# An attention stage's second product in column tiles of 32, with the sums as products of their own

## The chip, the cores and the metric

The kernel runs on one core of a Trainium2 chip. The metric is device time in microseconds (us) of one execution; a kernel's time is the median of its runs.

## What is computed

Attention over 2 batches of 12 heads, 448 positions and 64 values a head, with a soft cap on the scores, and then two feed-forward layers on the 896 tokens of 768 values. All inputs are 4-byte floats.

```
scores = (q @ k.T) / sqrt(64)            # per batch and head, 448 x 448
scores = cap * tanh(scores / cap)
attn   = exp(scores - max(scores)); attn = attn / (sum(attn) + 1e-9)
x      = attn @ v                        # heads joined: 896 x 768
h = x @ w_in;  x = (h * cos(h)) @ w_out      # 768 -> 2048 -> 768
h = x @ w_in2; out = (h * sigmoid(h)) @ w_out2
```

## The kernel before, in words

The order of the work on every engine is written out by hand; a tile framework adds the semaphores. After the attention stage come four projections (`gemm_in`, `gemm_out`, `gemm_in`, `gemm_last`), three matmuls for each product of split operands. Weights are prepared one after the other by `w_guard`, `w_floor`, `w_bits`, `w_hi` and `w_lo`; the first few of these steps are spread over the attention loop (the table `early`).

Attention works on 12 pairs of heads (`NPT`). A pair's two heads lie one above the other: head u of a pair takes rows 64u to 64u+63 of q and k, both stored with the 64 values of a head along the partitions and the positions along the free axis. Keys are the rows of a score tile, queries its 448 columns, so that the tile can be used as it stands in the second product. 448 keys make three whole tiles of 128 and a rest of 64 for each head; the rests of the two heads share one tile of 128 rows, the last keys (t = 3), in which k is stored so that the other head's rows are zero.

One turn of the loop over p (line 341) does the following.

- `load(p+3)` on GpSimd's queue and `load_v(p+1)` on SP's bring q and k (`raw`, three buffers) and v (`vf`).
- `S_pe(p+1, t)` on TensorE: q and k have been split into a high part `qh` and a low part `ql` of a reduced 4-byte type (`qk_split`, VectorE), and a score tile is three matmuls: high-high, high-low, low-high. For t = 0 to 2 each head has its own (64 rows, line 225, the two heads side by side), for t = 3 the two share one of 128 rows (line 228). Score tiles lie in three buffers of two banks each (`ps_s`), taken in turn, so that t = 3 takes the buffer of t = 0 of the same pair.
- `S_tanh(p+1, t)` and `S_exp(p+1)` on ScalarE write `e32`, seven chunks of 128 keys: chunk 2t+u for head u, chunk 6 for the last keys of both.
- `PV_mixed(p)`, between `S_pe(p+1, 2)` and `S_pe(p+1, 3)`, and `PV(p, u, ...)` at the turn's end are the second product, in plain 4-byte floats. Each head has its own accumulator (`po0`, `po1`, one bank each). The stationary operand is 128 columns wide: 64 values of v and, beside them, 64 columns of ones that were set once (`v_init`, GpSimd), so that the other half of the accumulator holds the sums of the exponentials, 64 times. Head u takes chunks u, u+2, u+4 with 128 rows and its 64 rows of chunk 6 in `PV_mixed`.
- `evac(p, u)` copies an accumulator to `xu` (VectorE, line 269) and sends one row of sums by SP's queue (line 271) to a small tile.
- `recip(p-2)`: reciprocal of the sums (line 277), to memory and back as a broadcast (`rs`, `rb`; lines 279 and 282, SP's queue). `norm_mul(p-3)` and `norm_split(p-3)` (lines 290, 297, 298, VectorE) multiply and split the result into `x`, which the first projection reads.

In the last turn there are no scores; `recip(10)` is brought forward, and the steps of pairs 9 to 11 follow the loop (lines 363 to 368). The first projection, `gemm_in`, reads batch 0 first (pairs 0 to 5) for two column tiles of the weights, then batch 1 without its last two pairs, and then pairs 10 and 11.

In a profile a 4-byte matmul of line 255 is two records of TensorE (and two weight loads), a matmul of the reduced type is one.

Of the kernel before, what the change touches and what calls it, by code (L numbers as in the profile page):

```python
# [25 lines left out]
F32 = mybir.dt.float32  # L28
F32R = mybir.dt.float32r
# [7 lines left out]
def tile_attention_ffn_ffn(  # L37
# [120 lines left out]
    with ExitStack() as actx:  # L158
# [5 lines left out]
        NCH = 7  # L164
        VW = 3 * D
        KB = S + 64
        QK = S + KB
        FIRST = S + P
        PAD = 16

        raw, vf = {}, []


        def v_init():
            for n in range(2):
                t = ap_.tile([P, NCH, VW], F32, name=f"vf{n}", bufs=1)
                nc.gpsimd.memset(t, 1.0)
                vf.append(t)

# [14 lines left out]
        def load_v(p):  # L194
            if p >= NPT:
                return
            nc.sync.dma_start(vf[p % 2][:, :, D:2 * D], qkv[p][:, PAD + QK:].rearrange("p (c d) -> p c d", d=D))

        qh, ql = {}, {}

        def qk_split(p, part=slice(0, QK)):
            if p >= NPT:
                return
            if p not in qh:
                qh[p] = ap_.tile([P, QK], F32R, tag="qh", name=f"qh{p}", bufs=2)
                ql[p] = ap_.tile([P, QK], F32R, tag="ql", name=f"ql{p}", bufs=2)
# [6 lines left out]
        def S_pe(p, t):  # L213
# [3 lines left out]
            sc[p, t] = ps  # L217
            h, l = qh[p], ql[p]
# [24 lines left out]

        po_ = {}
        wide = [slice(D, 3 * D), slice(0, 2 * D)]


        def PV(p, u, chunks):
            first = (p, u) not in po_
            if first:  # L250
                po_[p, u] = ps_o.tile([P, 512], F32, tag=f"po{u}", name=f"po{p}_{u}")[:, :S]
            for n, c in enumerate(chunks):
                rows = slice(0, P) if c < NCH - 1 else slice(u * D, (u + 1) * D)
                last = c < NCH - 1 and c >= NCH - 3
                nc.tensor.matmul(po_[p, u], vf[p % 2][rows, c, wide[u]], e32[p][rows, c, :], start=first and n == 0, stop=last)  # L255

        def PV_mixed(p):
            for u in range(2):
                PV(p, u, [NCH - 1])

        xu, sums, rb = {}, {}, {}

        def evac(p, u):
            if p < 0:
                return
            if u == 0:
                xu[p] = ap2.tile([P, 2, S], F32, tag="xu", name=f"xu{p}", bufs=4)
                sums[p] = ap2.tile([32, S // 16], F32, tag="sums", name=f"sums{p}", bufs=2)
            nc.vector.tensor_copy(xu[p][:, u], po_.pop((p, u)))
            row = D if u == 0 else 0  # L270
            nc.sync.dma_start(sums[p][16 * u:16 * u + 16], xu[p][row:row + 1, u, :])

        def recip(p):
            if p < 0:
                return
            s = sums.pop(p)
            nc.vector.reciprocal(out=s, in_=s)
            d = dpool.tile([2, S], F32, tag="rs", name=f"rs{p}")
            nc.sync.dma_start(d.rearrange("h (a n) -> (h a) n", a=16), s)
            r = ap2.tile([P, S], F32, tag="rb", name=f"rb{p}", bufs=4)  # L280
# [36 lines left out]
        nc.vector.memset(zero.bitcast(F32), 0.0)  # L317
        warm_up(8, ps_o.tile([P, 512], F32, tag="po1", name="warm0")[:, :S])

# [3 lines left out]
        get_scap(raw[0][:, :1])  # L323
        qk_split(0, slice(FIRST, QK))
        load(1)
# [11 lines left out]
        qk_split(1)  # L337
        warm_up(4, ps_o.tile([P, 512], F32, tag="po1", name="warm1")[:, :S])
        for u in range(2):
            PV(0, u, range(u, 4, 2))  # L340
        for p in range(NPT):
# [285 lines left out]
```

## Time and profile before

| | us |
|---|---|
| median of 3 runs | 579.0 (578.89 to 579.34) |
| the profiled execution | 579.33 |
| its span | 577.6 |
| TensorE busy | 571.5 (99%) |
| VectorE busy | 387.0 (67%) |
| ScalarE busy | 265.8 (46%) |
| GpSimd busy | 158.0 (27%) |
| granted clock of TensorE, mean over the span | 1.0 |

The span runs from the first instruction to the end of the last; the execution's own time is 1.7 us longer. Attention takes about the first 106 us of the span, the four projections the rest. A record of TensorE lasts longer than the distance to the next one, because matmuls are pipelined; the distance is what counts in a sum.

### The profile page before, as it was taken

The page shows a single profiled execution, that of the slowest core. Times are in us where ns is not written, and L with a number is a line of the kernel's source. Part 1 is how long each engine was busy: PE and PEld are TensorE (multiplying, and loading weights), DVE is VectorE, ACT ScalarE, POOL GpSimd, SP SyncE. Part 2 cuts the span into 40 slices and gives each one's busy share as a digit, 9 for nine tenths or more (in the row PEclk, how much of TensorE's full clock was granted, in tenths as well). Part 3 has the DMA queues.
Part 4 walks back from the last instruction along what each step waited for, and adds up shares of the span by engine and source line. Part 5 has one row for each costly group of instructions (what it writes and reads, how often), then busy time and mean ns, then how long its engine had stood idle before and what let it go on. Part 6 is the DMA issues. An engine that isn't in the chain of part 4 may idle for free.

```text
span 577.6 us, 7312 instructions
## 1 busy us (share of the span) xinstructions
PE 571.5 (99%) x2856; PEld 502.1 (87%) x2856; DVE 387.0 (67%) x490; ACT 265.8 (46%) x307; POOL 158.0 (27%) x81
## 2 busy tenths in 40 slices
PE   8999999999999999999999999999999999999997
PEld 5656655799999999999999999999999999999997
DVE  4358885599988898667646552888877776654501
ACT  5988888167777766223223222443333323232101
POOL 3001100033444433242332221344332323413300
PEclk9999999999999999999999999999999999999999
DMA  9236532123433333343433330343333334444102
GB/s 327 70 99 173 178 115 64 50 81 103 135 120 110 109 92 100 105 143 97 133 107 110 106 119 40 111 138 136 110 109 110 110 110 128 145 135 132 48 1 95
DMA packets 27201, 65.04 MB, mean 113 GB/s; under 512 B 14176, under 2 KB 17760, under 8 KB 27168
## 3 DMA queue, kind: packets, MB, share of 16 engines
q1 hardware_dynamic: 25728, 57.51, 31.9%
q0 software_dynamic: 1152, 6.78, 3.4%
q8 instruction: 22, 0.36, 0.2%
q10 hardware_dynamic: 288, 0.30, 0.2%
q14 instruction: 11, 0.09, 0.0%
HBM read 61.74 MB, written 2.80 MB: 112 GB/s over the span
## 4 chain that ended last, share of the span: by engine, by line
PE 98%; DMA 1%; DVE 0%; issue 0%; ACT 0%
PE h L397 40%; PE y L397 20%; PE o L544 20%; PE po L255 11%; PE sc L225 4%; PE sc L228 2%; DMA raw<-in_qkv 1%; PE warm L305 0%; DVE ql L209 0%; DVE qh L208 0%; DVE os L567 0%; ACT os L566 0%; DVE capt L71 0%
## 5 line engine op out<-in xcount | busy, mean ns | idle before, releaser
L119 POOL TENSOR_SCALAR w<-w 128x768 f32<-128x768 f32 (+1 forms) x63 | 148.4, 2355 | 312.5 <-ACT w L113 248.5
L397 PE MATMUL h<-x,whi 128*128 128x448 f32 x768 | 218.4, 366 | 0.0
L397 PEld LDWEIGHTS h<-x,whi 128*128 128x128 f32 x768 | 144.2, 188 | 11.8 <-issue 0.4
L397 PE MATMUL h<-x,wlo 128*128 128x448 f32 x384 | 140.2, 365 | 0.0
L143 ACT ACTIVATE whi<-w 128x768 fp32r<-128x768 f32 (+1 forms) x66 | 54.3, 822 | 143.2 <-DVE w L135 132.6
L544 PE MATMUL o<-whi,g 128*128 128x384 f32 x448 | 113.9, 335 | 0.0
L397 PE MATMUL y<-g,whi 128*128 128x448 f32 x384 | 109.3, 366 | 0.0
L132 DVE SCALAR_TENSOR_TENSOR w<-w,wraw 128x768 int32<-128x768 int32 (+1 forms) x66 | 61.5, 932 | 43.8 <-POOL w L119 42.9
L150 DVE TENSOR_TENSOR wlo<-w,whi 128x768 fp32r<-128x768 f32 (+1 forms) x66 | 61.4, 931 | 31.6 <-ACT whi L143 30.8
L544 PEld LDWEIGHTS o<-whi,g 128*128 128x128 f32 x448 | 81.0, 188 | 0.0
L397 PEld LDWEIGHTS y<-g,whi 128*128 128x128 f32 x384 | 72.1, 188 | 5.9
L397 PEld LDWEIGHTS h<-x,wlo 128*128 128x128 f32 x384 | 72.1, 188 | 5.7
L544 PE MATMUL o<-wlo,g 128*128 128x384 f32 x224 | 74.9, 335 | 0.0
L397 PE MATMUL y<-g,wlo 128*128 128x448 f32 x192 | 70.2, 366 | 0.0
L255 PE MATMUL po<-e,vf 128*128 128x448 f32 (+1 forms) x192 | 68.3, 541 | 1.0 <-issue 1.0
L135 DVE SCALAR_TENSOR_TENSOR w<-wraw,w 128x768 uint32<-128x768 uint32 (+1 forms) x66 | 61.6, 934 | 2.3
L130 DVE TENSOR_SCALAR wraw<-wraw 128x768 int32<-128x768 int32 (+1 forms) x66 | 55.9, 846 | 9.0 <-ACT w L113 9.0
L113 ACT ACTIVATE w<-wraw 128x768 f32<-128x768 f32 (+1 forms) x66 | 57.9, 877 | 2.7 <-DMA wraw<-in_moe_w_out 2.7
L255 PEld LDWEIGHTS po<-e,vf 128*128 128x128 f32 (+1 forms) x192 | 31.9, 189 | 25.9 <-issue 24.3
L236 ACT ACTIVATE e<-sc,scap 128x896 f32<-128x896 f32 (+1 forms) x48 | 40.8, 912 | 15.8 <-PE sc L225 11.8
L544 PEld LDWEIGHTS o<-wlo,g 128*128 128x128 f32 x224 | 42.1, 188 | 0.0
L453 ACT ACTIVATE r<-h 128x896 f32<-128x896 f32 (+1 forms) x18 | 14.8, 836 | 58.7 <-PE h L397 56.8
(53 smaller groups left out, 411.4 us busy)
## 6 DMA issues: line engine op xcount, KB each, us to landing
wraw<-in_moe_w_in SPq DMA_DIRECT2D x29, 768.0 KB, 4.3
wraw<-in_moe_w_out SPq DMA_DIRECT2D x22, 768.0 KB, 4.4
wraw<-in_moe_w_out SPq DMA_DIRECT2D x12, 640.0 KB, 4.1
raw<-in_qkv POOLq DMA_DIRECT2D x9, 480.0 KB, 6.3
vf<-in_qkv SPq DMA_DIRECT2D x12, 224.0 KB, 2.9
rb<-rs SPq DMA_DIRECT2D x24, 112.0 KB, 2.9
out<-os SPq DMA_DIRECT2D x13, 192.0 KB, 1.9
wraw<-in_moe_w_in POOLq DMA_DIRECT2D x3, 768.0 KB, 5.1
```

What stands on the lines that cost most here:

```text
L113: nc.scalar.activation(out=w32[i][:, :n, :].bitcast(F32), in_=wraw[i][:, :n, :, 1].bitcast(F32), func=AF.Abs, scale=2.0 ** -48)
L119: eng.tensor_scalar(out=t, in0=t, scalar1=2.0 ** -63, scalar2=None, op0=ALU.max)
L130: nc.vector.tensor_scalar(out=w1, in0=w1, scalar1=-0x80000000, scalar2=None, op0=ALU.bitwise_and)
L132: nc.vector.scalar_tensor_tensor(out=t, in0=t, scalar=3, in1=w1, op0=ALU.logical_shift_left, op1=ALU.bitwise_or)
L135: nc.vector.scalar_tensor_tensor(out=t, in0=w0.bitcast(U32), scalar=29, in1=t, op0=ALU.logical_shift_right, op1=ALU.bitwise_or)
L143: nc.scalar.activation(out=whi[i][:, :n, :], in_=w32[i][:, :n, :].bitcast(F32), func=AF.Copy)
L150: nc.vector.tensor_tensor(out=wlo[i][:, :n, :], in0=w32.pop(i)[:, :n, :].bitcast(F32), in1=whi[i][:, :n, :].bitcast(F32), op=ALU.subtract)
L225: nc.tensor.matmul(ps[:, u, :S], kk[rows, cols], qq[rows, :S], start=m == 0, stop=m == 2)
L236: nc.scalar.activation(out=e32[p][:, 2 * t:2 * t + n, :], in_=sc.pop((p, t))[:, :n, :S], func=AF.Tanh, scale=scap)
L255: nc.tensor.matmul(po_[p, u], vf[p % 2][rows, c, wide[u]], e32[p][rows, c, :], start=first and n == 0, stop=last)
L397: nc.tensor.matmul(pt, l, r, start=first and m == 0, stop=last and m == len(ops) - 1)
L544: nc.tensor.matmul(pt[t], l, r[:, cols], start=k == 0 and m == 0, stop=k == KF - 1 and m == 2)
```

## The change

The second product is cut into tiles of 32 columns of the array. A tile of 32 columns writes 32 partitions of the accumulator, so four matmuls with different tiles make up its 128 partitions. The two heads of a pair share one accumulator, `po`: partitions 0 to 63 for head 0, 64 to 127 for head 1. A step t of `PV` is four matmuls, each with 128 rows, 32 columns of v and the head's own chunk of `e32`; step 3 is the last keys, for which v is now stored twice (`NV` = 8 chunks), once for each head, with zeros in the other head's rows.

The sums are no longer columns of the stationary operand. `PV_sums` computes them with tiles of ones, 32 columns each, in a second accumulator, `sm`: two steps of four matmuls. The four quarters of `sm` are two partial sums for each head; `evac_sums` copies them, four transfers bring them to a small tile, and `recip` adds the two before the reciprocal.

The last keys' scores (`S_pe` with t = 3) are four matmuls of plain 4-byte floats, 32 columns each, straight from `raw`; the last keys are no longer split. `PV_mixed` is gone. `norm_mul` is one operation on 128 partitions in place of two on 64. In the last turn `PV_sums` and `evac_sums` come ahead of `PV`. `ones` is a tile of three times 32 columns.

```diff
-        VW = 3 * D
+        NV = NCH + 1
+        Q = 32
+        W = 32
+        FULL = S + S // P * P
+        ones = const.tile([P, 3, Q], F32, name="ones")
         def v_init():
-            for n in range(2):
-                t = ap_.tile([P, NCH, VW], F32, name=f"vf{n}", bufs=1)
-                nc.gpsimd.memset(t, 1.0)
-                vf.append(t)
+            nc.gpsimd.memset(ones[:, 0], 1.0)
+            for u in range(2):
+                for h in range(2):
+                    nc.gpsimd.memset(ones[h * D:(h + 1) * D, 1 + u], float(u == h))
...
-            nc.sync.dma_start(vf[p % 2][:, :, D:2 * D], qkv[p][:, PAD + QK:].rearrange("p (c d) -> p c d", d=D))
+            vf[p] = ap_.tile([P, NV, D], F32, tag="vf", name=f"vf{p}", bufs=2)
+            nc.sync.dma_start(vf[p].rearrange("p c d -> p (c d)"), qkv[p][:, PAD + QK:])
...
-        def qk_split(p, part=slice(0, QK)):
+        def qk_split(p, part=slice(0, FULL)):
...
             else:
-                for m, (kk, qq) in enumerate(ops):
-                    nc.tensor.matmul(ps[:, 0, :S], kk[:, S + 3 * P:S + 4 * P], qq[:, :S], start=m == 0, stop=m == 2)
+                x = raw[p][:, PAD:]
+                for c in range(0, P, W):
+                    nc.tensor.matmul(ps[c:c + W, 0, :S], x[:, FULL + c:FULL + c + W], x[:, :S], start=True, stop=True)
...
-        def PV(p, u, chunks):
-            first = (p, u) not in po_
+        def PV(p, steps):
+            first = p not in po_
             if first:
-                po_[p, u] = ps_o.tile([P, 512], F32, tag=f"po{u}", name=f"po{p}_{u}")[:, :S]
-            for n, c in enumerate(chunks):
-                rows = slice(0, P) if c < NCH - 1 else slice(u * D, (u + 1) * D)
-                last = c < NCH - 1 and c >= NCH - 3
-                nc.tensor.matmul(po_[p, u], vf[p % 2][rows, c, wide[u]], e32[p][rows, c, :], start=first and n == 0, stop=last)
-
-        def PV_mixed(p):
+                po_[p] = ps_o.tile([P, 512], F32, tag="po", name=f"po{p}")[:, :S]
+            for n, t in enumerate(steps):
+                for c in range(0, P, W):
+                    u, f = divmod(c, D)
+                    nc.tensor.matmul(po_[p][c:c + W], vf[p][:, 2 * t + u, f:f + W], e32[p][:, min(2 * t + u, NCH - 1), :],
+                                     start=first and n == 0, stop=t == 3)
+
+        def PV_sums(p, steps):
+            first = p not in sm_
+            if first:
+                sm_[p] = ps_o.tile([P, 512], F32, tag="sm", name=f"sm{p}")[:, :S]
+            for n, t in enumerate(steps):
+                for c in range(4):
+                    u, x = divmod(c, 2)
+                    chunk = 4 * t + 2 * x + u
+                    one = ones[:, 0] if chunk < NCH - 1 else ones[:, 1 + u]
+                    nc.tensor.matmul(sm_[p][c * Q:(c + 1) * Q], one, e32[p][:, min(chunk, NCH - 1), :], start=first and n == 0, stop=t == 1)
+
+        def evac(p):
+            xu[p] = ap2.tile([P, S], F32, tag="xu", name=f"xu{p}", bufs=4)
+            nc.vector.tensor_copy(xu[p], po_.pop(p))
+
+        def evac_sums(p):
+            x = ap2.tile([P, S], F32, tag="xs", name=f"xs{p}", bufs=2)
+            sums[p] = ap2.tile([32, 2, S // 16], F32, tag="sums", name=f"sums{p}", bufs=2)
+            nc.vector.tensor_copy(x[:3 * Q + 1], sm_.pop(p)[:3 * Q + 1])
             for u in range(2):
-                PV(p, u, [NCH - 1])
...
-            nc.vector.tensor_copy(xu[p][:, u], po_.pop((p, u)))
-            row = D if u == 0 else 0
-            nc.sync.dma_start(sums[p][16 * u:16 * u + 16], xu[p][row:row + 1, u, :])
+                for y in range(2):
+                    at = u * D + y * Q
+                    nc.sync.dma_start(sums[p][16 * u:16 * u + 16, y], x[at:at + 1])
...
-            nc.vector.reciprocal(out=s, in_=s)
+            nc.vector.tensor_tensor(out=s[:, 0], in0=s[:, 0], in1=s[:, 1], op=ALU.add)
+            nc.vector.reciprocal(out=s[:, 0], in_=s[:, 0])
...
-            for u in range(2):
-                rows = slice(u * D, (u + 1) * D)
-                nc.vector.tensor_tensor(out=rb[p][rows], in0=xu[p][rows, u], in1=rb[p][rows], op=ALU.mult)
+            nc.vector.tensor_tensor(out=rb[p], in0=xu.pop(p), in1=rb[p], op=ALU.mult)
...
-        for u in range(2):
-            PV(0, u, range(u, 4, 2))
+        PV(0, [0, 1])
+        PV_sums(0, [0])
         for p in range(NPT):
...
-            PV_mixed(p)
             S_pe(p + 1, 3)
...
-            for u in range(2):
-                PV(p, u, range(u if p else 4 + u, NCH - 1, 2))
-                evac(p, u)
+            if p == NPT - 1:
+                PV_sums(p, [0, 1])
+                evac_sums(p)
+            PV(p, range(4) if p else [2, 3])
+            evac(p)
+            if p < NPT - 1:
+                PV_sums(p, [0, 1] if p else [1])
+                evac_sums(p)
```

## Rows read from the trace of the kernel before

**Rows 1.** The page, busy us (share of the span) and instructions of an engine.
```profile
PE 571.5 (99%) x2856; PEld 502.1 (87%) x2856; DVE 387.0 (67%) x490; ACT 265.8 (46%) x307; POOL 158.0 (27%) x81
```

**Rows 2.** The page, the chain that ended last, by engine and by line.
```profile
PE 98%; DMA 1%; DVE 0%; issue 0%; ACT 0%
PE h L397 40%; PE y L397 20%; PE o L544 20%; PE po L255 11%; PE sc L225 4%; PE sc L228 2%; DMA raw<-in_qkv 1%; PE warm L305 0%; DVE ql L209 0%; DVE qh L208 0%; DVE os L567 0%; ACT os L566 0%; DVE capt L71 0%
```

**Rows 3.** Timeline of TensorE, one pair: start us, us, line, operation, shapes, count.
```profile
43.51 0.47 PE L225 MATMUL sc<-qh 64*128 64x448 f32 x2
...
45.23 0.37 PE L225 MATMUL sc<-qh,ql 64*128 64x448 f32 x2
45.44 0.92 PE L255 MATMUL po<-e,vf 64*128 64x448 f32 x4
46.28 0.47 PE L228 MATMUL sc<-qh 128*128 128x448 f32 x1
46.59 0.36 PE L228 MATMUL sc<-ql,qh 128*128 128x448 f32 x1
...
47.00 4.67 PE L255 MATMUL po<-e,vf 128*128 128x448 f32 x12
51.60 0.47 PE L225 MATMUL sc<-qh 64*128 64x448 f32 x2
```

**Rows 4.** Windows: busy us (instructions) of each engine, granted clock, DMA.
```profile
43.51:51.60 8.09, 8.09 (x38) 4.75 (x37) 7.05 (x11) 7.11 (x6) 1.59 (x3) 1.00 0.42 81
```

**Rows 5.** Timeline of ScalarE, the four tanh of that pair; idle before, releaser.
```profile
44.42 3.41 ACT L236 ACTIVATE e<-sc,scap 128x896 f32<-128x896 f32 x4 [1.74 <-PE sc L225]
```

**Rows 6.** Line 255's instructions: durations ns min/median/max, first and last start, forms.
```profile
L255 PE MATMUL po<-e,vf x192: 535/539/643, 10.5 to 106.1; 128*128 128x448 f32 x144, 64*128 64x448 f32 x48
```

**Rows 7.** Timeline of TensorE cut to 45.30 to 45.48, so first records only.
```profile
45.44 0.54 PE L255 MATMUL po<-e,vf 64*128 64x448 f32 x2
```

**Rows 8.** Timeline of VectorE, the last pair's multiplies and cast.
```profile
115.61 1.27 DVE L290 TENSOR_TENSOR rb<-xu,rb 64x448 f32<-64x448 f32 x2 [1.97 <-DMA rb<-rs]
116.92 0.40 DVE L297 CAST x<-rb 128x448 fp32r<-128x448 f32 x1
```

**Rows 9.** Timeline of SP's queue, issues of one pair, the first and the last.
```profile
84.10 1.18 SPq L271 DMA_DIRECT2D sums<-xu  x2
...
88.30 1.13 SPq L282 DMA_DIRECT2D rb<-rs  x2
```

**Rows 10.** The page, DMA issues: count, KB each, median us to landing.
```profile
raw<-in_qkv POOLq DMA_DIRECT2D x9, 480.0 KB, 6.3
```

**Rows 11.** Timeline of TensorE, first scores of the second and the fourth pair.
```profile
13.66 0.47 PE L225 MATMUL sc<-qh 64*128 64x448 f32 x2
...
27.32 0.47 PE L225 MATMUL sc<-qh 64*128 64x448 f32 x2
```

**Rows 12.** Timeline of ScalarE, the second pair's exp.
```profile
18.03 2.92 ACT L242 ACTIVATE e<-e,capt 128x3136 f32<-128x3136 f32 x1
```

**Rows 13.** Timeline of TensorE, narrow cuts: last records of pairs 10 and 11, a wait.
```profile
99.69 0.54 PE L255 MATMUL po<-e,vf 128*128 128x448 f32 x1
...
100.95 0.64 PE L255 MATMUL po<-e,vf 64*128 64x448 f32 x1
...
106.13 0.54 PE L255 MATMUL po<-e,vf 128*128 128x448 f32 x1
```

**Rows 14.** The chain in order of time, the first projection: start us, us, what.
```profile
106.67 116.75 PE h L397 x576
```

**Rows 15.** Timeline of SP's queue, the last two pairs' sums and an rb.
```profile
98.67 2.79 SPq L271 DMA_DIRECT2D sums<-xu  x2
...
107.12 1.08 SPq L282 DMA_DIRECT2D rb<-rs  x2
108.26 1.22 SPq L271 DMA_DIRECT2D sums<-xu  x2
```

**Rows 16.** Timeline of the weight loads, one of the last keys' scores.
```profile
46.60 0.19 PEld L228 LDWEIGHTS sc<-qh,ql 128*128 128x128 f32 x1
```

More of the change, by code (lines that the diff above doesn't have):

```diff
@@ L164, in tile_attention_ffn_ffn @@
         NCH = 7
-        VW = 3 * D
+        NV = NCH + 1
+        Q = 32
         KB = S + 64
         QK = S + KB
+        W = 32
+        FULL = S + S // P * P
         FIRST = S + P
         PAD = 16
-        raw, vf = {}, []
+        raw, vf = {}, {}
+        ones = const.tile([P, 3, Q], F32, name="ones")
         def v_init():
-            for n in range(2):
-                t = ap_.tile([P, NCH, VW], F32, name=f"vf{n}", bufs=1)
-                nc.gpsimd.memset(t, 1.0)
-                vf.append(t)
+            nc.gpsimd.memset(ones[:, 0], 1.0)
+            for u in range(2):
+                for h in range(2):
+                    nc.gpsimd.memset(ones[h * D:(h + 1) * D, 1 + u], float(u == h))
         def load(p):
@@ L204, in qk_split @@
             if p not in qh:
-                qh[p] = ap_.tile([P, QK], F32R, tag="qh", name=f"qh{p}", bufs=2)
-                ql[p] = ap_.tile([P, QK], F32R, tag="ql", name=f"ql{p}", bufs=2)
+                qh[p] = ap_.tile([P, FULL], F32R, tag="qh", name=f"qh{p}", bufs=2)
+                ql[p] = ap_.tile([P, FULL], F32R, tag="ql", name=f"ql{p}", bufs=2)
             h, x = qh[p][:, part], raw[p][:, PAD:][:, part]
@@ L217, in S_pe @@
             sc[p, t] = ps
-            h, l = qh[p], ql[p]
+            h, l = qh.get(p), ql.get(p)
             ops = ((h, h), (h, l), (l, h))
@@ L242, in S_exp @@
             nc.scalar.activation(out=e, in_=e, func=AF.Exp, scale=capt)
-        po_ = {}
-        wide = [slice(D, 3 * D), slice(0, 2 * D)]
-        def PV(p, u, chunks):
-            first = (p, u) not in po_
+        po_, sm_ = {}, {}
+        def PV(p, steps):
+            first = p not in po_
             if first:
-                po_[p, u] = ps_o.tile([P, 512], F32, tag=f"po{u}", name=f"po{p}_{u}")[:, :S]
-            for n, c in enumerate(chunks):
-                rows = slice(0, P) if c < NCH - 1 else slice(u * D, (u + 1) * D)
-                last = c < NCH - 1 and c >= NCH - 3
-                nc.tensor.matmul(po_[p, u], vf[p % 2][rows, c, wide[u]], e32[p][rows, c, :], start=first and n == 0, stop=last)
@@ L257, in PV_mixed @@
-        def PV_mixed(p):
-            for u in range(2):
-                PV(p, u, [NCH - 1])
[L261 to L268, printed above, removed]
-            nc.vector.tensor_copy(xu[p][:, u], po_.pop((p, u)))
-            row = D if u == 0 else 0
-            nc.sync.dma_start(sums[p][16 * u:16 * u + 16], xu[p][row:row + 1, u, :])
+                po_[p] = ps_o.tile([P, 512], F32, tag="po", name=f"po{p}")[:, :S]
@@ new lines, in tile_attention_ffn_ffn @@
+        xu, sums, rb = {}, {}, {}
+        def evac(p):
[5 more added lines that the diff above has]
+            nc.vector.tensor_copy(x[:3 * Q + 1], sm_.pop(p)[:3 * Q + 1])
+            for u in range(2):
+                for y in range(2):
+                    at = u * D + y * Q
+                    nc.sync.dma_start(sums[p][16 * u:16 * u + 16, y], x[at:at + 1])
@@ L276, in recip @@
             s = sums.pop(p)
-            nc.vector.reciprocal(out=s, in_=s)
+            nc.vector.tensor_tensor(out=s[:, 0], in0=s[:, 0], in1=s[:, 1], op=ALU.add)
+            nc.vector.reciprocal(out=s[:, 0], in_=s[:, 0])
             d = dpool.tile([2, S], F32, tag="rs", name=f"rs{p}")
-            nc.sync.dma_start(d.rearrange("h (a n) -> (h a) n", a=16), s)
+            nc.sync.dma_start(d.rearrange("h (a n) -> (h a) n", a=16), s[:, 0])
             r = ap2.tile([P, S], F32, tag="rb", name=f"rb{p}", bufs=4)
@@ L317, in tile_attention_ffn_ffn @@
         nc.vector.memset(zero.bitcast(F32), 0.0)
-        warm_up(8, ps_o.tile([P, 512], F32, tag="po1", name="warm0")[:, :S])
+        warm_up(8, ps_o.tile([P, 512], F32, tag="sm", name="warm0")[:, :S])
         nc.scalar.activation(out=scap, in_=zero[:, :1].bitcast(F32), func=AF.Tanh)
@@ L323, in tile_attention_ffn_ffn @@
         get_scap(raw[0][:, :1])
-        qk_split(0, slice(FIRST, QK))
+        qk_split(0, slice(FIRST, FULL))
         load(1)
@@ L337, in tile_attention_ffn_ffn @@
         qk_split(1)
-        warm_up(4, ps_o.tile([P, 512], F32, tag="po1", name="warm1")[:, :S])
-        for u in range(2):
-            PV(0, u, range(u, 4, 2))
+        warm_up(4, ps_o.tile([P, 512], F32, tag="sm", name="warm1")[:, :S])
+        PV(0, [0, 1])
+        PV_sums(0, [0])
         for p in range(NPT):
@@ L603 @@
     v = np.asarray(inputs["v"]).reshape(n, 2, S, D)
-    qkv = np.zeros((n, P, pad + S + full + 128 + 7 * D), np.float32)
+    qkv = np.zeros((n, P, pad + S + full + 128 + 8 * D), np.float32)
     qkv[:, :, 0] = inputs["cap"]
@@ L613 @@
             qkv[:, :, at:at + D] = v[:, u, c * 128:(c + 1) * 128]
-        qkv[:, u * 64:(u + 1) * 64, -D:] = v[:, u, full:]
+        at = pad + S + full + 128 + (6 + u) * D
+        qkv[:, u * 64:(u + 1) * 64, at:at + D] = v[:, u, full:]
     give("qkv", qkv)
```

## The prediction

> **What bounds the kernel now.** I read the page's busy shares first: TensorE (PE) is busy for 99% of the span [rows 1]. A high share can still hide waits, so the chain that ended last comes next: 98% of it is PE. Lines 225, 228 and 255, the attention stage that the change touches, are 17% of the chain; lines 397 and 544, 80%, lie behind it on the same engine and are left alone [rows 2]. So a microsecond of PE time taken out of the attention loop shortens the kernel, unless another engine becomes late there or the first projection has to wait for attention's last result. The third view is PE's own timeline of one pair, which gives the durations [rows 3]; the busy times of the other engines over the same stretch, and ScalarE's timeline, say how much room they have [rows 4, 5].
>
> **One pair before.** From pair to pair PE takes 8.09 us (43.51 to 51.60) [rows 3]. The scores of three key tiles are nine steps of two matmuls: the first step takes 0.31, the others 0.20, and the last streams for about 0.19: 1.91. Then the mixed second product, four records two by two. Records of line 255 follow each other every (4.67-0.54)/11 = 0.375, so this is 0.75. Then the last keys' scores, 0.31+0.20+0.20 = 0.71, and twelve records of the second product, 4.50. Between 64-row and whole-array tiles there is a gap of about 0.1, twice (45.44+0.75 to 46.28; 47.00+4.50 to 51.60). The sum is 8.07; 0.02 stays open.
>
> **One pair after.** A 4-byte matmul is two records (192 records for 12 x 8 matmuls), each of the same length whether it has 64 rows or 128 [rows 6]. Now the last keys' scores are one group of four such matmuls, the second product four groups and the sums two: seven groups of eight records, in place of 19 records. No row of before shows a tile of 32 columns. The bounds are set by how much runs side by side: all four matmuls, and a group is two record times, 0.75; none, and it is eight, 3.0. Below 0.75 nothing is expected: 448 columns still have to pass, and the rows show one record time for both tile heights. I take 0.75, by the nearest row: the mixed product is the only place where two 4-byte matmuls hold different tiles. Line 255 issues u = 0 with its two records, then u = 1; two records start together at 45.44 and all four end within 0.92 [rows 3, 7]. One after the other they would need 3 x 0.375 + 0.54 = 1.67. So the engine does run a later matmul's first record past an earlier matmul's second one. That is two row tiles; four column tiles that read the same 128 rows are the extrapolation.
>
> The Trainium skill speaks against this in TensorE: Matmul & The Clock Gate, section Step-by-step: what each phase is for: only weight loads are pulled ahead, the matmuls stay in program order. By that rule the second matmul of a group could start no earlier than the first one's second record, and the sum would be that of the pairs rival below. By that rule the mixed records could not start two by two, and they do, at 45.44, so for row tiles the trace doesn't agree; for column tiles no run here shows it.
>
> The other terms of the pair: the scores stay at 1.91 and the two gaps at 0.1 each; the first group behind a gap has no weights loaded ahead, 0.11 (0.31 against 0.20). 1.91 + 0.1 + 0.11 + 7 x 0.75 + 0.1 = 7.47, a gain of 0.62 a pair.
>
> **What lies beside it.** ScalarE's work is unchanged, 7.11 us in this stretch with one weight step [rows 4], under 7.47. The last keys' scores need the score buffer of tile 0 (there are three), so they wait for its tanh. That one starts 0.91 after the pair's first matmul and takes about 1.0 [rows 5], so it ends at 1.92; PE is ready at 2.01: nothing is lost, but only 0.1 covers it, where the mixed product stood between before. If the cover is gone, each 0.1 of lateness costs 12 x 0.1. VectorE loses one of two line 290 multiplies (half of 1.27 [rows 8]) and 128 of the split's 960 columns, gains one add on 32x28 values (under the 0.40 of a cast of 448 columns [rows 8]; I take 0.2), and keeps two evacuations: its 7.05 [rows 4] becomes about 6.6. If it were late by all that it has spare, an accumulator would still be empty before its next use, over 3 us later. SP's queue issues four sums transfers in place of two: a pair's issues, from the first sums to the last rb, take 5.33 with their waits, and two more at 0.59 make 6.5 of 7.47 [rows 9], hidden until the end. GpSimd loses a memset at the start, off the chain. Its loads of raw now wait for the last keys' scores instead of the split, about a pair later; they land in 6.3 [rows 10] and are needed over a pair and a half after: nothing. The weight loads queued behind them on GpSimd are used two pairs later or more.
>
> **Start.** Before, the second pair's scores start at 13.66 and the fourth's at 27.32 [rows 11]. After: from 10.45, two groups and one of sums end near 12.8, so scores at 12.9. ScalarE starts on them at 13.8 and, by its present lengths (3.4 [rows 5] and 2.9), ends that pair's exp at 20.2, before 20.95 [rows 12]. PE reaches the following last-key group at 20.1, but must wait for a tanh that only then starts, until 21.25; 0.11 + 5.25 + 0.1 from there puts the next scores at 26.75. The gain is 0.57; 0.9 of waiting for ScalarE takes the rest.
>
> **End.** Pair 10's products end at 100.07 (99.69 + 0.375), pair 11's at 106.51 (106.13 + 0.375): 6.44. After, pair 11's sums need the single sums bank, which VectorE has to empty first: 0.88, as in the wait before (100.07 to 100.95 [rows 13]), then 0.1 for a slow first record, 1.5 and 3.0: 5.48, a gain of 0.96. A change to whole-array tiles now stands ahead of the first projection: 0.2 lost.
>
> Then the tail. The projection reads pair 11's result after 63 matmuls of 0.203 (116.75/576 [rows 14]), with the 0.2 at 13.0 after the last product. Before, it was ready at 117.32, the end of the cast [rows 8], so 10.8 after it. SP takes in order: sums of pair 10, then rs and rb of pair 9, rs and rb of pair 10, sums of pair 11, its rs and rb [rows 15]. Two more sums of pair 10 push this by 1.9: at 0.61 each, four end 3.35 behind the product, and two ended at 101.46, 1.4 behind. Two more of pair 11 push by 1.22. PE's end moves 0.96 closer; the one multiply saves 0.64; the add costs 0.2. Ready at 10.8 + 0.96 + 1.9 + 1.22 - 0.64 + 0.2 = 14.4, so PE waits 1.4. Bounds 0 to 2.8: a chain of transfers whose spacing is known only for two.
>
> **The sum.** Start 0.57; nine pair times until pair 10's end, 9 x 0.62 = 5.58; 0.96; less 0.2; less 1.4: a gain of 5.51. The profiled execution took 579.33 (a span of 577.6 and 1.7 around it), so 573.8 in its terms; against the median of 579.0 it is 573.5. This forecast's own range is 571 (no wait in the tail, gaps a little smaller) to 577.
>
> **The rivals.** Three are prices of a group, times 12 x 7 = 84 groups.
> *Weights not hidden* (slower). Mechanism: in a column tile, the second record's weight load can't run under the first record's matmul. Place: every record in the new tiles. Price: 0.11 a record (an unhidden first load, above) up to 0.19 (a whole load [rows 16]), two in a row per group: 84 x 0.22 to 84 x 0.38, 18.5 to 32: 592 to 605. It decides from a group of 0.75 + 5.51/84 = 0.82, 0.03 a record. For it: no row shows such a load hidden. Against: a load for the same 128 rows runs beside a matmul now (46.60 [rows 16] beside 46.59 [rows 3]).
> The Trainium skill states a rule of this kind in TensorE: Matmul & The Clock Gate, section The mechanism: weight loads overlap matmuls in flight only where their row groups differ, and four column tiles share all rows. By that rule the time would be this rival's or worse; the load at 46.60 on equal rows doesn't agree with it.
> *Pairs only* (slower; the change doesn't do what it says). Matmuls keep their order, so each overlaps only its neighbour: a group is 4 x 0.375 = 1.5, and 84 x 0.75 = 63: 636. The start two by two speaks against it, but shows no more than two [rows 7].
> *No overlap* (slower). If four streams out of the same rows share one reading path, a group is 3.0: 84 x 2.25 = 189: 762. The mixed tiles read different rows, so nothing excludes it.
> *ScalarE takes the gain* (no change). A tanh late by 0.6 in every pair would put PE back to 8.09: 578 to 580. The 7.11 against 7.47 speaks against it.
>
> **How the numbers follow.** The forecast gets 0.60, weights not hidden 0.17, pairs 0.13, no overlap 0.06, ScalarE 0.04. 636 and 762 are the 0.19 that is left out, so the range is 570.5 to 605. About 0.2%, 1.2 us, is what a measurement of this kernel tells from no change: faster 0.59, same 0.05, slower 0.36.
>
> **What would show it.** Right: four records of a group starting together, groups 0.75 apart, pairs 7.4 to 7.5 apart, and a wait of about 1 us for pair 11 some 13 us into the first projection. Wrong: a group spacing of 0.97, 1.5 or 3.0 names the rival; late last-key scores name ScalarE; a longer wait in the projection names SP's queue.

## The result, and the profile after

| | before | after |
|---|---|---|
| median, us | 579.17 (578.89 to 579.35) | 583.78 (582.58 to 589.44) |
| the profiled execution, us | 579.33 | 589.44 |
| its span, us | 577.6 | 587.6 |
| TensorE (PE) busy, us | 571.5 | 573.7 |
| ratio of times after to before | | 1.0099, 95% interval 1.0071 to 1.0126 |

The kernel became about 1% slower; the forecast was 573.5, faster by 5.5. The profiled execution is the longest of the four runs of after; of its 10.1 us over before, 6.0 are a matter of their own (below) that the runs at 582.6 and 582.7, by their times, do not have.

The page of after: busy times, the granted clock in slices, and the chain that ended last.

```profile
PE 573.7 (98%) x3300; PEld 488.1 (83%) x3300; DVE 379.6 (65%) x490; ACT 265.4 (45%) x307; POOL 155.3 (26%) x84
...
PEclk9999999979999999999999999999999999999999
...
PE 83%; DMA 9%; DVE 3%; SPq 2%; ACT 1%; issue 1%; DVEq 0%
PE h L419 39%; PE y L419 20%; PE o L566 20%; DMA rs<-sums 4%; DMA rb<-rs 3%; SPq L290 2%; PE po L262 1%; DMA sums<-xs 1%; PE sc L232 1%; DVE rb L308 1%; ACT e L244 1%; SPq L302 1%; PE sm L275 1%; DMA raw<-in_qkv 1%; ACT e L250 0%
```

Before, the chain was 98% PE [rows 2]. Now 17% lie elsewhere, and the names say where: the transfers of the sums (`sums`, `rs`, `rb`), SP's queue that issues them, and VectorE's multiply (L308) that waits for the last one. PE's share of the attention stage has nearly gone from the chain. The clock row has one slice below 9 behind the start, the ninth (117.5 to 132.2).

TensorE's own work came as forecast. PE's timeline of after, from the last keys' scores (`sc<-raw`) to the next pair's first scores, and then (second fence) the same cut to 44.0 to 44.2, so that only first records are left.

```profile
44.05 0.96 PE L236 MATMUL sc<-raw 128*32 128x448 f32 x8
44.82 3.19 PE L262 MATMUL po<-e,vf 128*32 128x448 f32 x32
47.83 1.69 PE L275 MATMUL sm<-e,ones 128*32 128x448 f32 x16
49.45 0.47 PE L232 MATMUL sc<-qh 64*128 64x448 f32 x2
```

```profile
44.05 0.58 PE L236 MATMUL sc<-raw 128*32 128x448 f32 x4
```

All four matmuls of a group start together. The eight records of the last keys' scores take 0.77 with the first load (44.05 to 44.82), the 32 of the second product 3.01 (44.82 to 47.83), the 16 of the sums 1.52 plus the gap: groups of 0.75. From 36.60 to 44.05 a pair takes 7.45, before 8.09 [rows 3].

But the pairs do not all follow at 7.45. The places in PE's timeline of after where PE sat idle (in brackets: idle before, releaser) for more than 0.3 us in the loop, and the end of the attention stage:

```profile
21.71 0.96 PE L236 MATMUL sc<-raw 128*32 128x448 f32 x8 [0.85 <-ACT e L244]
...
53.39 3.21 PE L262 MATMUL po<-e,vf 128*32 128x448 f32 x32 [0.94 <-DVE ql L216]
...
77.27 3.21 PE L262 MATMUL po<-e,vf 128*32 128x448 f32 x32 [1.29 <-DVE xu L281]
...
98.40 1.71 PE L275 MATMUL sm<-e,ones 128*32 128x448 f32 x16 [1.57 <-DVE sums L296]
...
102.53 0.59 PE L262 MATMUL po<-e,vf 128*32 128x448 f32 x4
```

The first of these was in the forecast (0.9), and 0.88 of the last. The other two make two turns 8.59 and 8.92 long. The last product ends at 102.53+0.376 = 102.91, 3.6 before its end in before (106.51 [rows 13]); less the 0.2 that the forecast took for the tile change ahead of the first projection that is 3.4 instead of the 6.9 (0.57 + 5.58 + 0.96 - 0.2) in the sum. PE reaches the third matmul of the projection 3.4 earlier (103.55 against 106.93).

Where the stops come from is seen on SP's queue. Its timeline in after (issues, us each, count):

```profile
47.61 0.53 SPq L204 DMA_DIRECT2D vf<-in_qkv  x1
48.18 0.43 SPq L299 DMA_DIRECT2D rs<-sums  x1
53.73 1.13 SPq L302 DMA_DIRECT2D rb<-rs  x2
...
69.00 2.47 SPq L290 DMA_DIRECT2D sums<-xs  x4
...
72.54 1.08 SPq L299 DMA_DIRECT2D rs<-sums  x1
76.69 1.13 SPq L302 DMA_DIRECT2D rb<-rs  x2
77.91 2.44 SPq L290 DMA_DIRECT2D sums<-xs  x4
...
99.41 1.13 SPq L302 DMA_DIRECT2D rb<-rs  x2
100.64 2.43 SPq L290 DMA_DIRECT2D sums<-xs  x4
...
115.13 1.12 SPq L302 DMA_DIRECT2D rb<-rs  x2
```

One round, from one `sums` to the next, is 8.91 here (69.00 to 77.91): four issues, `vf`, `rs`, then the wait until `rs` has landed (72.54 to 76.69, 4.15), then `rb`, and only then the next `sums`, which stand behind `rb` in the queue. With an `rs` that lands in 2.4 the round is 6.7 (from the rb at 60.95 to that at 67.68). From the rb at 53.73 to that at 99.41 six rounds take 45.68, 7.61 each: more than PE's 7.45. The two rounds before these took 8.93 and 9.88 (`rb` at 34.92, 43.85 and 53.73), while PE still kept to 7.45. So the queue is as good as full: a quick round wins back 0.7, a slow one loses up to 2.4, and the lateness stays for several pairs. The groups of DMA issues in the window 45 to 55 of after (count, KB, median us to landing) show how slow one can be while `raw` and weights are on their way:

```profile
vf<-in_qkv SPq DMA_DIRECT2D x1, 256.0 KB, 5.6
...
rs<-sums SPq DMA_DIRECT2D x1, 3.5 KB, 5.5
```

That `vf`, issued at 47.61, lands at 53.2, and PE starts the product that reads it at 53.39. The view names VectorE's `ql` as the releaser of this stop (written from 52.31 to 53.33), but the product doesn't read it: that `ql` belongs to a later pair's scores. The same stop in the kernel of "The tail alone" below, which is the same up to the first projection, is put down to the v load itself:

```profile
52.74 3.21 PE L262 MATMUL po<-e,vf 128*32 128x448 f32 x32 [0.87 <-DMA vf<-in_qkv]
```

The stop at 77.27 goes by another way, VectorE's timeline:

```profile
74.97 0.62 DVE L308 TENSOR_TENSOR rb<-xu,rb 128x448 f32<-128x448 f32 x1 [3.42 <-DMA rb<-rs]
...
76.60 0.62 DVE L281 COPY xu<-po 128x448 f32<-128x448 f32 x1
...
118.94 0.63 DVE L308 TENSOR_TENSOR rb<-xu,rb 128x448 f32<-128x448 f32 x1 [3.60 <-DMA rb<-rs]
```

VectorE takes these operations in the program's order. The multiply of a pair three turns back waits for `rb`; behind it stands the evacuation of `po` (L281), whose product had ended at 71.4, and PE can't begin the next product before that. So a late broadcast of an old pair stops TensorE. Two things make this one late: its two transfers went out at 67.68 and 68.29, only 0.7 ahead of a product (68.35; with two transfers a pair, below, the same pair's go out from 60.85, 5.2 ahead of the product at 66.10), and they took 6.0 and 6.7 to land, where those of 60.95 took 2.8.

Then the tail: PE's timeline in the first projection, and windows (us, busy and instructions of PE, PEld, DVE, ACT, POOL, granted clock, DMA): two of after, and the second one's stretch in before.

```profile
115.72 0.36 PE L419 MATMUL h<-x,wlo 128*128 128x448 f32 x1
120.05 1.40 PE L419 MATMUL h<-x,whi 128*128 128x448 f32 x2 [3.97 <-DVE x L315]
...
125.70 0.37 PE L419 MATMUL h<-x,wlo 128*128 128x448 f32 x1
```

```profile
118.83:125.66 6.83, 5.61 (x14) 4.71 (x15) 6.51 (x11) 3.97 (x8) 1.97 (x1) 0.50 0.07 16
130.00:215.00 85.00, 85.00 (x413) 77.18 (x413) 74.39 (x85) 60.30 (x72) 34.34 (x12) 1.00 0.33 110
...
130.00:215.00 85.00, 85.00 (x421) 78.76 (x421) 76.85 (x86) 61.57 (x73) 34.07 (x12) 1.00 0.34 108
```

PE waits 4.1 (from 115.72+0.20 to 120.05) for the last pair's result. During that wait the granted clock falls to 0.50, the lower level (1.2 GHz), and stays there until 125.66: 14 matmuls take 5.65 instead of 14 x 0.203 = 2.84, so 2.8 more are lost. The second window belongs to the longest run alone: at full clock the matmuls of the third projection are 0.2067 apart instead of 0.2027 (576 of them take 119.03, in before 116.74), so 2% fewer stand in the same 85 us (413, in before 421).

The account of the profiled execution: -3.4 (attention ends earlier) + 4.1 (wait) + 2.8 (clock) + 6.0 (wider spacing from 125.7 to the end of the third projection, against the same matmuls in before) + 0.5 (the fourth projection, 117.06 against 116.55) = +10.0, where 10.1 was measured. The 0.5 is in the trace of every kernel with the new attention stage; why is not shown. Without the wider spacing it is +4.0, 583.3; two of the other runs lie 0.6 below that.

### The profile page after: what moved, and what is told of

It reads as the page before. It is cut to its first block, busy times and chain, and to the rows that moved or that the text cites. A ratio compares the mean times of both kernels' runs of the same rounds, so it can differ in the third digit from the quotient of the medians.

```text
span 587.6 us, 8250 instructions
## 1 busy us (share of the span) xinstructions
PE 573.7 (98%) x3300; PEld 488.1 (83%) x3300; DVE 379.6 (65%) x490; ACT 265.4 (45%) x307; POOL 155.3 (26%) x84
## 4 chain that ended last, share of the span: by engine, by line
PE 83%; DMA 9%; DVE 3%; SPq 2%; ACT 1%; issue 1%; DVEq 0%
PE h L419 39%; PE y L419 20%; PE o L566 20%; DMA rs<-sums 4%; DMA rb<-rs 3%; SPq L290 2%; PE po L262 1%; DMA sums<-xs 1%; PE sc L232 1%; DVE rb L308 1%; ACT e L244 1%; SPq L302 1%; PE sm L275 1%; DMA raw<-in_qkv 1%; ACT e L250 0%
## 5 line engine op out<-in xcount | busy, mean ns | idle before, releaser
L419 PE MATMUL h<-x,whi 128*128 128x448 f32 x768 | 222.8, 371 | 4.0 <-DVE x L315 4.0
L419 PE MATMUL h<-x,wlo 128*128 128x448 f32 x384 | 142.1, 370 | 0.0
L262 PE MATMUL po<-e,vf 128*32 128x448 f32 x384 | 38.6, 540 | 2.2 <-DVE xu L281 1.3
L419 PEld LDWEIGHTS y<-g,wlo 128*128 128x128 f32 x192 | 36.0, 188 | 3.6
```

Of the source, the lines that this page charges most:

```text
L262: nc.tensor.matmul(po_[p][c:c + W], vf[p][:, 2 * t + u, f:f + W], e32[p][:, min(2 * t + u, NCH - 1), :], start=first and n == 0, stop=t == 3)
L419: nc.tensor.matmul(pt, l, r, start=first and m == 0, stop=last and m == len(ops) - 1)
```

## The experiments

The theory (Q in the expectations): the two more transfers a pair fill SP's queue, and stops, tail wait and fallen clock all follow from that. Rivals: the landings of more transfers, not their issue; something in the new tiles (spacing, clock); the last product's place next to the projection.

**The transfers without the tiles.** The kernel before, each of its two transfers cut in two.

```diff
-            nc.sync.dma_start(sums[p][16 * u:16 * u + 16], xu[p][row:row + 1, u, :])
+            for y in range(2):
+                at = 16 * u + 8 * y
+                nc.sync.dma_start(sums[p][at:at + 8], xu[p][row:row + 1, u, y * S // 2:(y + 1) * S // 2])
```

> The kernel before, with each of its two sums transfers cut into two of half a row: four transfers a pair, nothing else changed. Theory Q: before had 2.0 us to spare for pair 11 and now loses 1.9 + 1.2 of it to SP's queue, so PE waits about 1 us in the first projection; 579.5 to 581, and 583 if the clock falls in that wait. Rival L: no change, 578.9 to 579.4.

Measured: 582.28, ratio 1.0049 [1.0032, 1.0066]. SP's queue at the last pair's sums, PE in the projection, and the window of the lower clock, in this kernel:

```profile
110.71 2.72 SPq L273 DMA_DIRECT2D sums<-xu  x4
```

```profile
119.02 0.36 PE L399 MATMUL h<-x,wlo 128*128 128x448 f32 x1
121.11 0.47 PE L399 MATMUL h<-x,whi 128*128 128x448 f32 x1 [1.74 <-DVE x L299]
```

```profile
122.43:125.84 3.41, 3.41 (x11) 3.04 (x10) 3.29 (x6) 3.09 (x6) 1.06 (x1) 0.50 0.00 0
```

Two more transfers a pair cost 3.2 us (579.12 was before's median beside it) with nothing else changed. In the loop there is no stop, because a pair here lasts 8.09; in the tail PE waits 1.9 (119.22 to 121.11), where about 1 was expected. In the profiled run (583.26) the clock is then at the lower level: 11 matmuls take 3.41 instead of 2.23. It is not in every run: of the four, two have a mean granted clock of 0.996 (582.70 and 583.26), two of 1.000 (581.69 and 581.85, 0.7 and 0.9 above the 579.5 to 581 expected without a fall). In the profiled run the fall costs 1.2. The last pair's sums go out at 110.71 instead of 108.26 [rows 15].

**The tiles without the transfers.** After, with the partial sums laid out so that one transfer takes two rows, one for each head.

```diff
-                    u, x = divmod(c, 2)
+                    x, u = divmod(c, 2)
...
-            for u in range(2):
-                for y in range(2):
-                    at = u * D + y * Q
-                    nc.sync.dma_start(sums[p][16 * u:16 * u + 16, y], x[at:at + 1])
+            for y in range(2):
+                nc.sync.dma_start(sums[p][32 * y:32 * y + 32], x[D * y:D * y + Q + 1:Q])
```

> The changed kernel, with a pair's four sums transfers made into two of two rows each (the partial sums are laid out so that one transfer takes two of them); PE's work is the same. Theory Q (SP's queue: four sums transfers a pair at 0.61 us each, in order with rs and rb, fill the 7.45 us of a pair and make the last result late): the wait of 4.3 us before pair 11's part of the first projection goes, pairs stay at 7.45 without the stop at 77 us, TensorE's clock stays at full, and the whole time is 571 to 574. Rival L (the last turn itself is too tight: sums of pair 11 wait for the sums bank, and reciprocal, multiply and split come behind one another, whatever the number of transfers): the wait stays at 3 to 4 us and the time at 580 to 584.

Measured: 571.75 (571.64 to 573.24), ratio 0.9877 [0.9862, 0.9891]. SP's queue over one round; the chain in order of time (start us, us, what) over the last pairs; PE's last stop.

```profile
71.51 1.18 SPq L288 DMA_DIRECT2D sums<-xs  x2
...
73.64 0.33 SPq L297 DMA_DIRECT2D rs<-sums  x1
75.85 1.14 SPq L300 DMA_DIRECT2D rb<-rs  x2
79.10 1.16 SPq L288 DMA_DIRECT2D sums<-xs  x2
...
105.87 1.16 SPq L300 DMA_DIRECT2D rb<-rs  x2
```

```profile
81.15 3.01 PE po L262 x32
...
88.56 3.01 PE po L262 x32
...
98.63 116.94 PE h L417 x576
```

```profile
93.91 1.71 PE L275 MATMUL sm<-e,ones 128*32 128x448 f32 x16 [0.84 <-DVE xs L286]
```

`rb` is out at 76.99, the next `sums` wait until 79.10 for VectorE's copy: the queue has 2.1 to spare. Behind the start there is no stop in the loop but the last pair's, and none in the tail; the clock stays at 1.00. The chain is PE alone, pairs 7.41 apart (81.15 to 88.56). This is the forecast's sum without a wait in the tail (572.1) within 0.4. The last `rb` goes out 9.3 earlier than in after (105.87, 115.13), while the projection starts only 4.5 earlier (98.56, 103.05).

**One transfer of four rows.**

```diff
-            for u in range(2):
-                for y in range(2):
-                    at = u * D + y * Q
-                    nc.sync.dma_start(sums[p][16 * u:16 * u + 16, y], x[at:at + 1])
+            nc.sync.dma_start(sums[p], x[:3 * Q + 1:Q])
```

> As the first experiment, but with one sums transfer of four rows in place of two of two rows. Theory Q says that SP's queue no longer sets any wait with two transfers, so nothing is left to gain: 571.3 to 572.2, the same as with two. If SP still set something, about 0.6 us a pair in part of the pairs and 0.6 in the tail would show: below 570.

Measured: 572.07, ratio 0.9872 [0.9859, 0.9884], the same as with two. Once the queue has room, less of it brings nothing.

**Four transfers, two of them on GpSimd's queue.**

```diff
-                    nc.sync.dma_start(sums[p][16 * u:16 * u + 16, y], x[at:at + 1])
+                    (nc.gpsimd if u else nc.sync).dma_start(sums[p][16 * u:16 * u + 16, y], x[at:at + 1])
```

> The changed kernel with all four sums transfers of a pair, two of them issued by GpSimd's queue in place of SP's. Theory Q (what is short is the time of SP's queue, where each issue takes 0.6 us and the rb issues wait for rs to land): SP is back to two sums issues, the stops of the attention loop and the long wait for pair 11 go, 571.5 to 574. Rival N (what costs is the number of small transfers and their landings, whoever issues them): four transfers still land late, 578 to 584.

Measured: 572.66 (571.57, 572.08, 573.24 and 578.39), ratio 0.9903 [0.9868, 0.9939]. The same four transfers land, only their issue is shared; so the rival of the landings falls. A slow landing still occurs (an `rs` issued at 66.12 is followed by its `rb` only at 70.93), but no stop comes of it. The profiled execution is the 578.39 one. SP's and GpSimd's timelines, and a window of the first projection:

```profile
72.19 1.18 SPq L290 DMA_DIRECT2D sums<-xs  x2
```

```profile
71.87 1.16 POOL L290 DMA_DIRECT2D sums<-xs  x2 [5.67 <-DVE sums L296]
```

```profile
130.00:215.00 85.00, 85.00 (x413) 77.21 (x412) 75.34 (x84) 60.82 (x71) 32.66 (x13) 1.00 0.32 105
```

Between the start and the last pair it has no stop, nowhere behind the start a lower clock, and still shows the wider spacing of the longest run of after, from its first projection on: the spacing needs no fallen clock.

**The clock alone.** After, with 20 matmuls ahead of those that read pairs 10 and 11, whose result is not used, so that PE works through most of the wait.

```diff
+        early_p = ps_tile(f"h{base}_2")
+        if base == 0:
+            for _ in range(20):
+                nc.tensor.matmul(early_p[:, 0, :S], whi[0][:, 0], xt[0][0][:, 0, :], start=True, stop=True)
```

> The changed kernel with 20 matmuls on ready operands (their results are overwritten) put on TensorE where it waits for pair 11, about 4.1 us of work in the place of an idle 4.1. Theory C (the wait costs more than its length: the clock falls to half for 6.8 us behind it, 3 us lost, and the projections behind run at 207 ns a matmul in place of 203, 6.5 us lost in the profiled run): the clock stays full, the matmuls stay at 203, and the time is 579 to 580.5. Rival (the slow 207 has another cause, and the clock's fall is the same without the wait): no gain, 582 to 585.

Measured: 579.14 (577.05 to 586.84 in ten runs), ratio 0.9998 [0.9977, 1.002], within the expectation; the profiled run took 581.63. PE's timeline and the window around it:

```profile
115.23 4.22 PE L508 MATMUL h<-x,whi 128*128 128x448 f32 x20
...
120.68 0.47 PE L419 MATMUL h<-x,whi 128*128 128x448 f32 x1 [0.63 <-DVE x L315]
```

```profile
115.00:125.00 10.00, 9.18 (x44) 7.93 (x44) 5.58 (x10) 2.68 (x5) 0.68 (x1) 1.00 0.06 23
```

PE is at the same matmul as in after (120.05) only 0.6 later, and the clock is 1.00 throughout: filling the wait with work gives the 2.8 of the clock back. That is read from this one profile; the runs spread too widely for their median (4.6 under after) to be a measure of it. A part of the expectation, that the wider spacing follows from the fallen clock, is not borne out: the kernel above shows it without a fall, and the kernel before with four transfers shows a fall without it (its spacing stays at 0.2027).

**The tail alone.** After, with the first two column tiles of batch 1 reading pairs 4 and 5 in place of 10 and 11.

```diff
-            mm3(pt[1][:, fc, :S], base + fc, xr(range(kc, KD), 1), False, True)
+            mm3(pt[1][:, fc, :S], base + fc, xr(range(kc, KD), 0 if base == 0 else 1), False, True)
```

> The changed kernel, in which the first projection takes pairs 4 and 5 in place of pairs 10 and 11 for its first two column tiles of batch 1, so that part of the product is computed from other data: the wait for the last pair is gone, all else is as it was, the four transfers too. Theory Q with C: the wait of 4.1, the half clock and the slow projections go together; what is left is the gain of the attention stage, 3.4 us as it ended in the trace: 575 to 576.5. Rival: the loss lies in the attention stage or in the projections themselves: 580 or more.

Measured: 577.16 (573.6 to 579.42 in ten runs), ratio 0.9957 [0.9937, 0.9977]. 6.6 under after, near the 4.1 + 2.8 of wait and clock, but above the expectation, which had already counted the stops in the loop (they remain: turns of 8.52, 7.89 and 8.67). In the profiled run (576.82) 1.1 come back at 124.68 and 125.67 as waits for weights. The spread is too wide to settle the last microsecond.

**Which part of the gain is whose.** First the last keys' scores as before, the rest as in the kernel with two transfers:

```diff
-        FULL = S + S // P * P
+        FULL = QK
...
-                x = raw[p][:, PAD:]
-                for c in range(0, P, W):
-                    nc.tensor.matmul(ps[c:c + W, 0, :S], x[:, FULL + c:FULL + c + W], x[:, :S], start=True, stop=True)
+                for m, (kk, qq) in enumerate(ops):
+                    nc.tensor.matmul(ps[:, 0, :S], kk[:, S + 3 * P:S + 4 * P], qq[:, :S], start=m == 0, stop=m == 2)
```

> The first experiment's kernel (two sums transfers) with the last keys' scores as before: three matmuls of split operands over the whole array, and all 960 columns split. PE by the rows: 0.71 in place of 0.86, and one more change of tiles between these scores and the second product, 0.1 for the gap and up to 0.11 for weights not loaded ahead: 0 to 0.06 a pair more, so 571.5 to 572.5; VectorE's 0.2 a pair is covered. Rival (a change between a whole-array tile and a 32-column one costs as much as the four-column group): 574 or more.

Measured: five runs at 572.31 to 573.65, seven at 578.74 to 579.18, median 578.75, ratio 0.9951 [0.9921, 0.9982]. The profiled one is of the lower group (572.58): a pair takes 7.49 (41.34 to 48.83), 0.06 more than with the new scores, as expected. The median is not: it lies in the upper group, and in the rival's range. The two groups lie 6.5 apart, which is what the wider spacing costs the kernel with GpSimd's queue (its first three projections take 357.15, those of the kernel with two transfers 350.68); that the upper group has the wider spacing is inferred, since none of it was profiled. The rival's dearer change of tile would lengthen the pair; the pair's 7.49 speaks against it.

Then the second product in tiles of 64 columns, two side by side:

```diff
-                for c in range(0, P, W):
-                    u, f = divmod(c, D)
-                    nc.tensor.matmul(po_[p][c:c + W], vf[p][:, 2 * t + u, f:f + W], e32[p][:, min(2 * t + u, NCH - 1), :],
+                for u in range(2):
+                    nc.tensor.matmul(po_[p][u * D:u * D + D], vf[p][:, 2 * t + u], e32[p][:, min(2 * t + u, NCH - 1), :],
```

> The first experiment's kernel with the second product in tiles of 64 columns, two side by side (one for each head), the sums and the last keys' scores still in 32. If a record takes 0.376 at any tile width and all tiles of one mode run together, the second product is still 3.0 a pair, and two more changes of tile mode in each pair cost 0.1 to 0.2 each: 2.4 to 4.8 in all, 574 to 576.5. If tiles of 64 columns did not run side by side, the second product would double: 36 us more, 608.

Measured: 575.5, ratio 0.9931 [0.9918, 0.9944]. PE's timeline:

```profile
46.01 3.23 PE L261 MATMUL po<-e,vf 128*64 128x448 f32 x16
49.16 1.71 PE L274 MATMUL sm<-e,ones 128*32 128x448 f32 x16
```

Two matmuls side by side, in the same four steps, take as long as four of half the width: 3.15 from start to start, the 0.14 over 3.01 being the change of tiles. What costs (3.75 over the kernel with two transfers, 0.27 to 0.3 a pair) are the two changes of tile, not the width.

**The spacing.** Before, with one group of four 32-column matmuls directly ahead of the first projection.

```diff
+        if base == 0:
+            for c in range(0, P, 32):
+                nc.tensor.matmul(pt[1][c:c + 32, 0, :S], whi[0][:, 0, c:c + 32].bitcast(F32), xt[0][0][:, 0, :].bitcast(F32), start=True, stop=True)
```

> The kernel before with one group of four 32-column matmuls of plain 4-byte floats put directly ahead of the first projection (their result is overwritten). Question: some runs of kernels with column tiles show the projections' 448-column matmuls 0.2067 us apart instead of 0.2027, from the first projection on and with the clock full (about 6.5 us in all). Theory A, a change from column tiles to whole-array tiles is enough to begin that spacing: the kernel before, which has shown it in none of its runs, now shows it in some: single runs at 586 to 587 beside others at 580. Theory B, it needs something else of the changed attention stage: all runs at 580.0 to 580.5, that is the kernel before plus the price of one group between whole-array tiles: 0.75 for the group, 0.1 for each gap and 0.03 to 0.1 for a first weight load.

Measured: 580.07 (579.94 to 580.7 in eleven runs), ratio 1.0015 [1.0006, 1.0024]: the price of one group, 0.8, and no run with 6.6 more. A change from column tiles to whole-array tiles is not enough to begin the wider spacing.

## Why the prediction was wrong

**What was right.** The group of four at 0.75 (0.752 measured), the first load, the gaps, the pair at 7.47 (7.45 here, 7.41 to 7.45 with two transfers), the wait of 0.9 for ScalarE at the start (0.85), the turn of the last pair (a stop of 0.84 against 0.88 once the queue has room), and no lateness of the last keys' scores in the later turns. The extrapolation from two row tiles to four column tiles held, and with it three rivals fell: loads not hidden, pairs only, no overlap. The fourth, ScalarE, shows in no turn behind the start. Here the Trainium skill's TensorE: Matmul & The Clock Gate, section Step-by-step: what each phase is for, differs from the trace, if the two records of a matmul stand one behind the other in the program, as the calls do: by program order the four first records couldn't start together, and they do, at 44.05. So does the sentence of its section The mechanism that the prediction used: by it tiles that share all rows would load in the open, and 32 records with a load each take 3.01, which is 8 x 0.376 with nothing between. The same section also lets a load go ahead into a background weight buffer, and that way the trace does not contradict. Where they differ, the measurement decides.

**The step that failed** is in "What lies beside it": SP's queue, "two more at 0.59 make 6.5 of 7.47, hidden until the end". It was sized on one pair [rows 9], in which `rs` landed quickly (issued at 85.99, its `rb` at 88.30). The trace of before already had slow ones, hidden only by the room that two transfers left; SP's queue in before:

```profile
69.83 0.48 SPq L279 DMA_DIRECT2D rs<-sums  x1
74.15 1.41 SPq L282 DMA_DIRECT2D rb<-rs  x2
```

Here the wait is 4.3, and the pair's issues, from the `sums` at 67.92, last 7.64 and not 5.33; with two more at 0.59 that is 8.8, over 7.47. A round has a wait for a landing inside, and in after landings of 2.4 to 5.5 make the round 6.7 to 9.9: 7.6 in the mean of the last six against 7.45. So the 1.0 to spare was not there. The row's number was right for its pair; that it was taken as the length of every round was the mistake. From this one step follow, in the profiled run, the three terms that the sum lacked:

- Stops in the loop: 1.14 (`vf` late) and 1.47 (`rb` late, evacuation behind it), and the last pair's stop 1.57 instead of 0.88: 3.3 of the attention stage's 6.9 gone. The prediction gave the evacuation over 3 us of cover for a VectorE that is slow itself, not for a multiply ahead of it that waits for `rb` (3.42 here), and it did not name `vf` behind `rb` on SP's queue.
- The tail: the chain was placed rightly, but from a queue that is on time. The sums of pair 10 go out about 3 late (four done at 103.07 against 3.35 behind a product that ends near 96.7), so that PE waits 4.1 instead of 1.4, outside the bounds of 0 to 2.8.
- The clock: a wait in the tail was costed at its own length. Behind 4.1 of idling it cost 2.8 more. No row of before shows a fall behind the start, so the sum had no term for it.

573.8 + 3.5 + 2.7 + 2.8, and the 0.5 of the fourth projection, make 583.3; two of the runs of after lie 0.6 below. That 583.8 still lies inside the range of 570.5 to 605 is luck: the range was drawn that far for weights that are not hidden, which the trace does not show. The sign of the forecast was lost on a resource off the chain that was costed at nothing; the prediction's own line for this ("a longer wait in the projection names SP's queue") is what the profile shows. A rival "SP's queue becomes the bound" was missing: with a spare of 1.0 a round and landings that vary by 2 in the trace of before, it had a place there.

The kernel with two transfers beats both: 571.75, 1.2% under before.

## What to carry to other kernels

A queue that waits for landings between its issues has no fixed round: take its length from many turns, with the slow landings in it, and compare it with the new, shorter period of the engine that you speed up. When work is taken off the bounding engine, ask of each in-order queue what stands behind its longest wait; here a broadcast of an old pair held up the evacuation that TensorE needed next. And count a wait of TensorE at more than its length where the trace shows the clock fall behind such a wait.

## What was not expected of the hardware

- At full granted clock, whole-array matmuls of 448 columns run at one of two spacings, 0.2027 or 0.2067 us. The wider one was seen in the profiled runs of after (from 125.7) and of the kernel with GpSimd's queue (from the first projection), holds on through three projections, and costs 6.0 and 6.5; the fourth, with 384 columns a matmul, takes 117.06 with it and 117.08 without (kernel with two transfers). It was seen only in kernels with the new attention stage, and not in all of their runs; neither a fallen clock nor a change from column tiles alone brings it. What begins it stays open.
- The clock fell behind idling of 4.1 (half clock for 6.8, from 118.83, still within the wait) and behind idling of 1.9 (for 3.4, in the profiled run of the kernel before with four transfers; by its mean clock in one more of the four runs). It did not fall behind the idling of 0.9 to 1.6 in the loop.
- A group of four 32-column tiles of 4-byte floats costs what a single such matmul does (0.75), and one more group between whole-array tiles 0.8.
- In the loop of after a transfer of 3.5 KB (`rs`) took 2.4 to 5.5 to land. From 31 to 99 us, its four slow landings (3.5 to 5.5) were issued 0.8 to 3.7 behind a load of `raw` on GpSimd's queue, the five quick ones (2.4 to 2.5) with no such load in the 5 us before. That the load is the cause was not tested.
